# Softplus in one function behind attention, and a conversion of weights whose clamp and add may run on GpSimd or VectorE

## The chip, the core and the metric

The kernel runs on one core of a Trainium2 chip. The core has TensorE (PE: matrix products, with weight loads shown apart as PEld), VectorE (DVE), ScalarE (ACT), GpSimd (POOL) and SyncE (SP), each with its own in-order queue; they wait for each other through semaphores. SP issues most DMAs, POOL a few. [...] The metric is the device time of one execution in microseconds, as the median of the runs.

## The reference

Three layers follow one another. Attention has 4 batches, 8 heads, 576 positions, head size 64, and a mask by blocks of 64. The first experts map 2304 rows of 512 to 2048 features and back, with a softplus between. The second experts normalize by the root mean square, make a gate and a value of 1536 features each, and map silu(gate) x value back to 512.

```python
scores = scale * np.matmul(q, k.transpose(0, 1, 3, 2))      # scale = 1/8
scores = np.where(mask, scores, -1000000000.0)
scores = scores - np.max(scores, axis=-1, keepdims=True)
attn = np.exp(scores)
attn = attn / (np.sum(attn, axis=-1, keepdims=True) + 1e-09)
x = attn @ v
...
h = x @ w_in
g = np.maximum(h, 0.0) + np.log1p(np.exp(-np.abs(h)))
y = g @ w_out
...
rms = np.sqrt(np.mean(y * y, axis=-1, keepdims=True) + 1e-06)
xn = y / rms * rms_g
g = xn @ w_gate
silu = g * (1.0 / (1.0 + np.exp(-g)))
out = (silu * (xn @ w_val)) @ w_out
```

## The kernel before, in words

**Stages.** The rows are cut into 6 blocks of 384, the 2048 features into 16 pieces of 128 (f), of which 9 (NA) belong to stage A and 7 to stage B, since the converted weights of 16 pieces don't fit beside attention's buffers. Stage A runs f = 0 to 8 for all blocks and is mixed with attention, block by block. Stage B, behind it, runs f = 9 to 15 for all blocks, 42 steps, adds what stage A left, takes the mean square and the reciprocal root of each row (`evac_b`), and stores the block. Then come the second experts: `load_xn` loads and normalizes a block, `g34` makes the products and the gate, `g5` the map back.

**Precision.** Products of the first experts and most of attention take a high and a low part of each operand, three products for one. Attention's first 12 of 48 units (`whole(u)`) take full fp32 operands instead: there k is used as loaded (`k0`), the score's maximum is scaled by 1/8 by an operation of its own (L769), and Exp scales by 1/8 (`s_exp`, L791).

**Conversion of weights.** They arrive as 64-bit words. `to_fp32` turns 128x512 of them into fp32 bits in six instructions: Abs of the high word (ACT, L470), conversion of the low word to an integer (ACT, L471), a clamp from below (DVE, L472), shift and mask (DVE, L464), the sign (DVE, L468), and the integer add of the low part (POOL, L475). It is done 68 times: 32 for the first experts' pieces (`w_unit`), 24 for gate and value (`gv_unit`), 12 for the last map (`o_pair`).

**Softplus.** `g1` makes h in a PSUM bank; then Abs (ACT, L963, from PSUM), Exp (L964), Ln of 1 + e (L965), and max(h, 0) + e on DVE (L966, from the same bank). The high part is copied by ACT (L331), the low part is a difference on DVE (L341); `g2` multiplies them three steps later (LAG). `evac_b` takes the root with Ln and Exp (L1030, L1031).

**What sets the order.** Nothing runs in the order of the code. `Plan` collects the operations with an engine, a cost, a key and their reads and writes; `schedule` walks through them, each engine taking the ready operation of the lowest key, and `emit` writes them in the order of their planned start. Where an operation lists several engines (`op2`, `aop2`, `small`), the planner takes the one that ends first by its costs. So a new cost or a new choice moves instructions on all engines. `after=` names operations that must have started before. ACT's functions lie in tables: a function outside the loaded one brings an ACT_TABLE_LOAD in front of it. Before, one table serves Abs, Copy, Square, Exp and Ln up to the first Silu.

## Time and profile before

| | us |
|---|---|
| median of 3 runs (lowest, highest) | 1015.72 (1014.25, 1019.61) |
| the profiled execution, its span | 1021.46, 1019.7 |
| PE busy in the span | 966.8 (95%) |
| DVE, ACT, POOL busy | 799.8 (78%), 658.2 (65%), 277.3 (27%) |
| weight loads busy | 841.0 (82%) |
| mean granted TensorE clock | 0.983 of full speed |

A busy share is a mean over stages with different limits. Attention and stage A reach to about 440 us, stage B to about 590, where the last of its steps overlap the first of the second experts; behind 640 us only these run. Idle time of an engine costs something only where the others wait for it; PE has the least.

### The profile page before, as it was taken

How to read it: one execution, taken by the hardware profiler on the slowest of the kernel's cores; microseconds unless marked ns; L12 is line 12 of the kernel's file. 1: busy time of each engine (PE TensorE's matmuls, PEld its weight loads, DVE VectorE, ACT ScalarE, POOL GpSimd, SP SyncE). 2: the span in 40 equal slices, each digit the busy share in tenths (PEclk: the TensorE clock that was granted, in tenths of full speed). 3: DMA queues.
4: the chain of work that ended last, by engine and by line, in shares of the span. 5: the costliest groups of instructions: out<-in, count | busy, mean ns of one | idle time of the engine just before them, and what ended most of it. 6: DMA issues, size and time to landing. Idle time of an engine off the chain costs nothing.

```text
span 1019.7 us, 20047 instructions
## 1 busy us (share of the span) xinstructions
PE 966.8 (95%) x7438; PEld 841.0 (82%) x7438; DVE 799.8 (78%) x1819; ACT 658.2 (65%) x1491; POOL 277.3 (27%) x353
## 2 busy tenths in 40 slices
PE   6888998899999999999999966999999999999998
PEld 4576887789899999999999966678778788788785
DVE  6889987788989858788687999899888754545545
ACT  7898776587878858787677776465565544333332
POOL 3544432222233303342322536232222110000000
PEclk9999999999999999999999989899999999999999
DMA  7354699999875442555664436052511200035422
GB/s 275 128 177 149 176 263 225 225 271 234 250 174 151 101 102 101 186 192 205 235 245 176 139 115 234 22 197 86 179 56 71 73 1 32 11 105 190 162 72 84
DMA packets 123315, 154.80 MB, mean 152 GB/s; under 512 B 85840, under 2 KB 93776, under 8 KB 121168
## 3 DMA queue, kind: packets, MB, share of 16 engines
q1 hardware_dynamic: 122640, 147.22, 47.9%
q0 software_dynamic: 576, 6.29, 1.7%
q8 instruction: 58, 0.95, 0.4%
q14 instruction: 41, 0.34, 0.1%
HBM read 101.19 MB, written 31.85 MB: 130 GB/s over the span
## 4 chain that ended last, share of the span: by engine, by line
PE 73%; DVE 10%; DMA 8%; ACT 6%; issue 2%; SPq 0%; POOL 0%; ACTq 0%; DVEq 0%
PE b L438 73%; DMA wraw<-in_w2gv_dram 3%; DMA wraw<-in_w_dram 2%; DMA raw<-in_vP_dram 1%; DMA raw<-in_kT_dram 1%; DVE pst L816 1%; DVE nm L757 1%; ACT P L791 1%; DVE g L341 1%; DVE w L551 1%; ACT P L835 1%; DVE t L966 1%; DMA pt<-pst 1%; DVE wa L468 1%; DVE tops L510 1%
## 5 line engine op out<-in xcount | busy, mean ns | idle before, releaser
L438 PE MATMUL b<-x,w 128*128 128x192 f16 (+1 forms) x4176 | 491.9, 273 | 14.2 <-ACT m L1106 6.1
L438 PEld LDWEIGHTS <-w 128*128 128x128 f16 x3024 | 252.7, 98 | 22.8 <-issue 14.1
L438 PE MATMUL b<-g,w 128*128 128x384 f32 x1152 | 234.3, 346 | 7.3 <-DVE g L341 3.6
L438 PEld LDWEIGHTS b<-g,w 128*128 128x128 f32 x1152 | 204.5, 192 | 13.0 <-DVE g L341 5.6
L438 PEld LDWEIGHTS b<-x,w 128*128 128x128 f32 x1152 | 199.6, 188 | 7.5 <-DVE nm L799 1.2
L438 PE MATMUL b<-w,g 128*128 128x512 f16 x648 | 147.6, 383 | 0.0
L438 PEld LDWEIGHTS <-g 128*128 128x128 f16 x648 | 63.4, 99 | 69.7 <-issue 2.4
L1106 ACT COPY m<-b 128x384 f32<-128x384 f32 x108 | 51.2, 477 | 81.9 <-PE b L438 81.7
L791 ACT ACTIVATE P<-b,nm 128x288 f32<-128x288 f32 (+8 forms) x160 | 79.7, 500 | 27.8 <-DVE nm L757 7.3
L1095 DVE TENSOR_TENSOR m<-m 128x384 f32<-128x384 f32 x64 | 37.9, 592 | 68.9 <-ACT m L1106 68.2
L475 POOL TENSOR_TENSOR wa<-wa,wraw 128x512 int32<-128x512 int32 x44 | 63.8, 1450 | 88.9 <-DVE wa L468 51.7
L757 DVE TENSOR_REDUCE nm<-b 128x1 f32<-128x288 f32 (+8 forms) x160 | 70.6, 449 | 16.1 <-PE b L438 14.2
L438 PE MATMUL b<-khl,qbd 128*128 128x448 f32 (+7 forms) x360 | 69.5, 314 | 4.4 <-ACT P L791 3.7
L341 DVE TENSOR_TENSOR g<-t,g 128x384 fp32r<-128x384 f32 x96 | 65.5, 684 | 8.5 <-ACT g L331 8.2
L816 DVE SCALAR_TENSOR_TENSOR pst<-P,nm,pst 128x128 f16<-128x128 f32 (+4 forms) x108 | 66.3, 626 | 3.3 <-ACT pst L813 2.5
L966 DVE SCALAR_TENSOR_TENSOR t<-b,t 128x384 f32<-128x384 f32 x96 | 52.7, 551 | 18.0 <-ACT t L965 17.6
L963 ACT ACTIVATE t<-b 128x384 f32<-128x384 f32 x96 | 46.8, 490 | 30.9 <-PE b L438 30.7
L438 PEld LDWEIGHTS b<-khl,qbd 128*128 128x128 f32 x360 | 57.1, 190 | 7.9 <-ACT P L791 5.4
L331 ACT CAST g<-t 128x384 fp32r<-128x384 f32 x96 | 48.9, 513 | 14.5 <-DVE t L966 11.1
L475 POOL TENSOR_TENSOR wg<-wg,wraw 128x512 int32<-128x512 int32 x24 | 34.3, 1431 | 87.3 <-DVE wg L468 67.0
L964 ACT ACTIVATE t<-t 128x384 f32<-128x384 f32 x96 | 50.4, 528 | 1.4
L965 ACT ACTIVATE t<-t 128x384 f32<-128x384 f32 x96 | 50.3, 527 | 1.2
(133 smaller groups left out, 1404.7 us busy)
## 6 DMA issues: line engine op xcount, KB each, us to landing
wraw<-in_w2gv_dram SPq DMA_DIRECT2D x48, 512.0 KB, 4.0
wraw<-in_w_dram SPq DMA_DIRECT2D x32, 512.0 KB, 3.3
wraw<-in_w2o_dram SPq DMA_DIRECT2D x24, 512.0 KB, 3.4
yd<-y SPq DMA_DIRECT2D x12, 768.0 KB, 4.1
y<-yd SPq DMA_DIRECT2D x12, 768.0 KB, 5.0
qf<-in_qP_dram SPq DMA_DIRECT2D x42, 192.0 KB, 3.1
xd<-x SPq DMA_DIRECT2D x4, 1536.0 KB, 7.4
x<-xd POOLq DMA_DIRECT2D x4, 1536.0 KB, 7.7
```

What stands on the lines that cost most here:

```text
L331: "ACT": ("ACT", t_act(n), lambda: nc.scalar.copy(dst(), src())),
L341: "DVE": ("DVE", t_dve(n), lambda: nc.vector.tensor_tensor(dst(), a(), b(), ALU.subtract)),
L438: nc.tensor.matmul(o, lhsT=l, rhs=r, start=start, stop=stop, **kw)
L475: op("POOL", t_pool2(CW), prio, lambda: nc.gpsimd.tensor_tensor(a().bitcast(I32), a().bitcast(I32), lw().bitcast(I32), ALU.add), [cell, (r ...
L757: aop("DVE", t_dve(cn), key, lambda sp=sp, col=col, cn=cn: nc.vector.tensor_reduce(nm()[:, col:col + 1], sp()[:, :cn], axis=AX.X, op=ALU.m ...
L791: aop("ACT", 0.24 + cn * 0.836e-3, key, lambda sp=sp, col=col, c0=c0, cn=cn: nc.scalar.activation(P()[:, c0:c0 + cn], sp()[:, :cn], ACTF.E ...
L816: aop("DVE", t_dve(c, True), key, lambda: nc.vector.scalar_tensor_tensor(lo(), pc(), r(), hi(), ALU.mult, ALU.subtract), [P, (P, "pad"), ( ...
L963: op("ACT", t_act(BLK, False), key - 5, lambda: nc.scalar.activation(e(), h()[:, :BLK], ACTF.Abs), [h], [e])
L964: op("ACT", t_act(BLK), key - 5, lambda: nc.scalar.activation(e(), e(), ACTF.Exp, scale=-1.0), [e], [e])
L965: op("ACT", t_act(BLK), key - 5, lambda: nc.scalar.activation(e(), e(), ACTF.Ln, bias=1.0), [e], [e])
L966: op("DVE", t_dve(BLK), key - 5, lambda: nc.vector.scalar_tensor_tensor(e(), h()[:, :BLK], 0.0, e(), ALU.max, ALU.add), [h, e], [e])
L1106: op("ACT", t_act(BLK, False), key + 1, lambda o=o, s=s: nc.scalar.copy(s(), ps(o)()), [o], [s])
```

## The change

Softplus, one function, stands in stage B in place of Abs, Exp, Ln and L966; stage A keeps them. It lies in another table, without Abs, Exp and Ln; so `evac_b` loads the table of Ln and Exp in front of its root and the next Softplus loads its own again, and a conversion that is planned for stage B takes the absolute value as a bitwise AND on DVE (`plain`). The first Softplus may start only when all Exps have. In `to_fp32` the clamp may go to POOL or DVE, and the add to POOL or DVE. For attention's first units k is scaled by 1/8 when it has come, and the scaling of the maximum and of Exp goes. Two single-column operations (L700, L799) may go to POOL too. In all, the order has 35 clamps on POOL and 33 on DVE, 28 adds on POOL and 40 on DVE, 38 ANDs on DVE and 30 Abs on ACT, 42 Softplus, 58 of 144 norms (L799, now L808) on POOL, and 14 table loads where there were 2.

```diff
@@ -449,6 +449,7 @@
...
     w_units = {}
+    plain = [0]
 
@@ -467,12 +468,21 @@
...
 
-        op("ACT", t_act(CW), prio, lambda: nc.scalar.activation(a(), hw().bitcast(FP32), ACTF.Abs), [raw], [cell])
         op("ACT", t_act(CW), prio, lambda: nc.scalar.activation(lw().bitcast(I32), lw(), ACTF.Copy, scale=2.0**-29), [raw], [(raw, "l")])
-        op("DVE", t_dve2(CW), prio, lambda: nc.vector.tensor_scalar(a(), a(), 2.0**-15, None, ALU.max), [cell], [cell], port=True)
+        if plain[0]:
+            op("DVE", t_dve2(CW), prio, lambda: nc.vector.tensor_scalar(a().bitcast(U32), hw(), 0x7FFFFFFF, None, ALU.bitwise_and), [raw], [cell])
+        else:
+            op("ACT", t_act(CW), prio, lambda: nc.scalar.activation(a(), hw().bitcast(FP32), ACTF.Abs), [raw], [cell])
+        op2([
+            ("POOL", t_pool(CW), lambda: nc.gpsimd.tensor_scalar(a(), a(), 2.0**-15, 2.0**-15, ALU.max, ALU.max)),
+            ("DVE", t_dve2(CW), lambda: nc.vector.tensor_scalar(a(), a(), 2.0**-15, None, ALU.max)),
+        ], prio, [cell], [cell], port=True)
         op("DVE", t_dve2(CW), prio, shift, [cell], [cell], port=True)
         op("DVE", t_dve(CW), prio, sign, [cell, raw], [cell], port=True)
-        op("POOL", t_pool2(CW), prio, lambda: nc.gpsimd.tensor_tensor(a().bitcast(I32), a().bitcast(I32), lw().bitcast(I32), ALU.add), [cell, (raw, "l")], [cell])
+        op2([
+            ("POOL", t_pool2(CW), lambda: nc.gpsimd.tensor_tensor(a().bitcast(I32), a().bitcast(I32), lw().bitcast(I32), ALU.add)),
+            ("DVE", t_dve(CW), lambda: nc.vector.tensor_tensor(a().bitcast(I32), a().bitcast(I32), lw().bitcast(I32), ALU.add)),
+        ], prio, [cell, (raw, "l")], [cell])
 
@@ -636,6 +646,7 @@
...
         att_ops.append(load(key, lambda: k0(p), kT[0, p], writes=[k_cell(p)], nbytes=294912))
+        aop2([("ACT", t_act(S), lambda: nc.scalar.mul(k0(p), k0(p), 0.125)), ("POOL", t_pool(S), lambda: nc.gpsimd.tensor_scalar(k0(p), k0(p), 0.125, 1.0, ALU.mult, ALU.mult))], key, [k_cell(p)], [k_cell(p)])
 
@@ -697,7 +708,7 @@
...
         aop("DVE", 0.07, key, lambda: nc.vector.tensor_scalar(dsc[p], am()[:, 1:2], 2.0**-28, None, ALU.mult), [am], [("dsc", p)])
-        aop("DVE", 0.07, key, lambda: nc.vector.tensor_scalar(am()[:, 2:3], am()[:, 1:2], 2.0**-14, None, ALU.mult), [am], [(am, "r")])
+        small(("POOL", "DVE"), lambda e: e.tensor_scalar(am()[:, 2:3], am()[:, 1:2], 2.0**-14, 1.0, ALU.mult, ALU.mult), key, [am], [(am, "r")])
         aop("DVE", 0.08, key, lambda: nc.vector.reciprocal(am()[:, 2:3], am()[:, 2:3]), [(am, "r")], [(am, "r")])
@@ -765,8 +776,6 @@
...
                 todo, i0, i1 = [done[-1]], ib, ib + 1
-            cells = [(nm, i) for i in range(i0, i1)]
-            small(("DVE", "POOL"), lambda e: e.tensor_scalar(nm()[:, i0:i1], nm()[:, i0:i1], 0.125, 1.0, ALU.mult, ALU.mult), key, cells, cells)
         else:
@@ -783,12 +792,12 @@
...
         P = part[u, ib] = R_P.new()
-        scale = 0.125 if whole(u) else 1.0
         if n % 128:
...
             col = 4 + ib + c
-            aop("ACT", 0.24 + cn * 0.836e-3, key, lambda sp=sp, col=col, c0=c0, cn=cn: nc.scalar.activation(P()[:, c0:c0 + cn], sp()[:, :cn], ACTF.Exp, scale=scale, bias=nm()[:, ib:ib + 1], accum_out=nm()[:, col:col + 1]), [sp, (nm, ib)], [P, (nm, "s", ib)])
+            exp_op.append(len(plan.ops))
+            aop("ACT", 0.24 + cn * 0.836e-3, key, lambda sp=sp, col=col, c0=c0, cn=cn: nc.scalar.activation(P()[:, c0:c0 + cn], sp()[:, :cn], ACTF.Exp, bias=nm()[:, ib:ib + 1], accum_out=nm()[:, col:col + 1]), [sp, (nm, ib)], [P, (nm, "s", ib)])
         if len(chunks) == 2:
@@ -796,7 +805,7 @@
...
         cells = [(nm, "s", i) for i in range(i0, i1)]
-        small(("DVE",), lambda e: e.tensor_scalar(nm()[:, 8 + i0:8 + i1], nm()[:, 4 + i0:4 + i1], 1e-9, 1.0 if whole(u) else 2.0**-14, ALU.add, ALU.mult), key, cells, [(nm, "t", i0)])
+        small(("DVE", "POOL"), lambda e: e.tensor_scalar(nm()[:, 8 + i0:8 + i1], nm()[:, 4 + i0:4 + i1], 1e-9, 1.0 if whole(u) else 2.0**-14, ALU.add, ALU.mult), key, cells, [(nm, "t", i0)])
         aop("DVE", 0.08, key, lambda: nc.vector.reciprocal(nm()[:, 12 + i0:12 + i1], nm()[:, 8 + i0:8 + i1]), [(nm, "t", i0)], [(nm, "r", i) for i in range(i0, i1)])
@@ -945,7 +954,9 @@
...
 
-    def g1(j, f, key):
+    exp_op, sp_op = [], []
+
+    def g1(j, f, key, soft=False):
         w, x, h = w_units["w1", f], x_b[j], R_h.new()
@@ -960,10 +971,15 @@
...
         g_b[j, f] = g
-        op("ACT", t_act(BLK, False), key - 5, lambda: nc.scalar.activation(e(), h()[:, :BLK], ACTF.Abs), [h], [e])
-        op("ACT", t_act(BLK), key - 5, lambda: nc.scalar.activation(e(), e(), ACTF.Exp, scale=-1.0), [e], [e])
-        op("ACT", t_act(BLK), key - 5, lambda: nc.scalar.activation(e(), e(), ACTF.Ln, bias=1.0), [e], [e])
-        op("DVE", t_dve(BLK), key - 5, lambda: nc.vector.scalar_tensor_tensor(e(), h()[:, :BLK], 0.0, e(), ALU.max, ALU.add), [h, e], [e])
+        if soft:
+            op("ACT", t_act(BLK, False) + (1.28 if not sp_op else 0.0), key - 5, lambda: nc.scalar.activation(e(), h()[:, :BLK], ACTF.Softplus), [h], [e], after=sp_op[-1:] or exp_op)
+            sp_op.append(len(plan.ops) - 1)
+        else:
+            op("ACT", t_act(BLK, False), key - 5, lambda: nc.scalar.activation(e(), h()[:, :BLK], ACTF.Abs), [h], [e])
+            op("ACT", t_act(BLK), key - 5, lambda: nc.scalar.activation(e(), e(), ACTF.Exp, scale=-1.0), [e], [e])
+            exp_op.append(len(plan.ops))
+            op("ACT", t_act(BLK), key - 5, lambda: nc.scalar.activation(e(), e(), ACTF.Ln, bias=1.0), [e], [e])
+            op("DVE", t_dve(BLK), key - 5, lambda: nc.vector.scalar_tensor_tensor(e(), h()[:, :BLK], 0.0, e(), ALU.max, ALU.add), [h, e], [e])
         op2(copies(nc, BLK, lambda: g()[:, 0], e, ("ACT",)), key - 2, [e], [(g, 0)])
@@ -1027,8 +1043,13 @@
...
         op("DVE", t_dve(BLK), key, lambda: nc.vector.tensor_scalar(ms(), o()[:, :BLK], 1.0 / DM, 1e-6, ALU.mult, ALU.add), [o], [ms])
-        op("ACT", t_act(BLK), key, lambda: nc.scalar.activation(rs(), ms(), ACTF.Ln), [ms], [rs])
-        rs_op[:] = [op("ACT", t_act(BLK), key, lambda: nc.scalar.activation(rs(), rs(), ACTF.Exp, scale=-0.5), [rs], [rs])]
+
+        def root():
+            nc.scalar.preload_act_table_set("natural_log_exp_and_others")
+            nc.scalar.activation(rs(), ms(), ACTF.Ln)
+            nc.scalar.activation(rs(), rs(), ACTF.Exp, scale=-0.5)
+
+        rs_op[:] = [op("ACT", 2 * t_act(BLK) + 2.56, key, root, [ms], [rs])]
         pair2(key, t, rs, rs, ALU.mult, [rs], [t])
@@ -1112,7 +1133,7 @@
...
         e1 = R_t.new()
-        op("ACT", t_act(BLK, False) + 0.09 + (1.28 if first else 0.0), key + 2, lambda: nc.scalar.activation(e1(), ps(A)(), ACTF.Silu, scale=fac(3)), [A, ("f", 3)], [e1], after=rs_op if first else ())
+        op("ACT", t_act(BLK, False) + 0.09 + (1.28 if first else 0.0), key + 2, lambda: nc.scalar.activation(e1(), ps(A)(), ACTF.Silu, scale=fac(3)), [A, ("f", 3)], [e1], after=rs_op + sp_op[-1:] if first else ())
         val1, gate2 = R_t.new(), s7
@@ -1272,6 +1293,7 @@
...
     t_b = win[NB] + LAG * step
+    plain[0] = 1
     for i, f in enumerate(range(NA, NF1)):
@@ -1307,7 +1329,7 @@
...
                 load_x(order[n + 1], key_b(s))
-            g1(j, f, key_b(s))
+            g1(j, f, key_b(s), True)
         if LAG <= s < n_b + LAG:
@@ -1333,6 +1355,7 @@
...
                 if i0 == 0 and 0 < n < len(late):
+                    plain[0] = 0
                     w2_unit(late[n], R_wB, key)
```

ACT in stage B, two steps of the activation before (t is the step's tile, b its bank; L471 and L331 are parts of the conversion and the high copy).

```order
L963 ACTIVATE t<-b_5998 128x384
L964 ACTIVATE t<-t 128x384
L965 ACTIVATE t<-t 128x384
L470 ACTIVATE wg<-wraw 128x512
L963 ACTIVATE t<-b_6019 128x384
L331 CAST g<-t 128x384
L964 ACTIVATE t<-t 128x384
L471 ACTIVATE wraw<-wraw 128x512
L965 ACTIVATE t<-t 128x384
L331 CAST g<-t 128x384
```

The same engine and place now, with the first table load of Softplus.

```order
L975 ACT_TABLE_LOAD
L975 ACTIVATE t<-b_5741 128x384
L471 ACTIVATE wraw<-wraw 128x512
L331 CAST w<-wa 128x512
L331 CAST g<-t 128x384
L975 ACTIVATE t<-b_5758 128x384
L331 CAST w<-wa 128x512
L331 CAST g<-t 128x384
L975 ACTIVATE t<-b_5780 128x384
L331 CAST g<-t 128x384
```

One instruction per step reads the bank where one of ACT and one of DVE did, and Abs of the conversion (L470) is gone from ACT.

ACT at the last block's root, before the first Silu (L1115, now L1136), before.

```order
L470 ACTIVATE wg<-wraw 128x512
L471 ACTIVATE wraw<-wraw 128x512
L1030 ACTIVATE r<-r 128x384
L1031 ACTIVATE r<-r 128x384
L1115 ACT_TABLE_LOAD
L1115 ACTIVATE t<-b_7698,fac 128x384
```

And now.

```order
L471 ACTIVATE wraw<-wraw 128x512
L560 ACTIVATE w<-wa,fac 128x512
L1048 ACT_TABLE_LOAD
L1049 ACTIVATE r<-r 128x384
L1050 ACTIVATE r<-r 128x384
L1136 ACT_TABLE_LOAD
L1136 ACTIVATE t<-b_7557,fac 128x384
```

A second load stands in front of the root; the one before Silu was there.

DVE behind the normalization of the first block of the second experts (L1052, now L1073, is a low part of it, L551, now L561, a weight's), before.

```order
L1052 TENSOR_TENSOR x<-y,x 128x384 x2
L472 TENSOR_SCALAR wa<-wa 128x512
L1011 TENSOR_TENSOR y<-y 128x2x192
L464 TENSOR_SCALAR wa<-wa 128x512
L551 SCALAR_TENSOR_TENSOR w<-wg,fac,w 128x256
L468 SCALAR_TENSOR_TENSOR wa<-wraw,wa 128x512
L1052 TENSOR_TENSOR x<-y,x 128x384
L472 TENSOR_SCALAR wa<-wa 128x512
L551 SCALAR_TENSOR_TENSOR w<-wg,fac,w 128x512
L464 TENSOR_SCALAR wa<-wa 128x512
```

And now (L473 is the AND, L478 the clamp, L465 the shift, L469 the sign, L484 the add).

```order
L473 TENSOR_SCALAR wa<-wraw 128x512
L1027 TENSOR_TENSOR y<-y 128x2x192
L478 TENSOR_SCALAR wa<-wa 128x512
L1073 TENSOR_TENSOR x<-y,x 128x384 x2
L465 TENSOR_SCALAR wa<-wa 128x512
L1027 TENSOR_TENSOR y<-y 128x2x192
L469 SCALAR_TENSOR_TENSOR wa<-wraw,wa 128x512
L561 SCALAR_TENSOR_TENSOR w<-wa,fac,w 128x512
L1073 TENSOR_TENSOR x<-y,x 128x384
L484 ISA wa<-wraw,wa 128x1024
L473 TENSOR_SCALAR wa<-wraw 128x512
L561 SCALAR_TENSOR_TENSOR w<-wg,fac,w 128x1024
```

The AND and the add have come into DVE's row, with the add written over 128x1024 half words; here the clamps stay on DVE.

## Rows read from the trace of the kernel before

**Rows 1.** Stretches: length, busy PE, PEld, DVE, ACT, POOL, clock, DMA share, GB/s.

```profile
30.00:100.00 70.00, 60.92 (x356) 47.51 (x355) 60.34 (x171) 63.79 (x156) 30.68 (x40) 0.97 0.46 154
100.00:300.00 200.00, 186.72 (x1401) 171.50 (x1400) 172.40 (x524) 147.09 (x393) 61.83 (x114) 0.98 0.91 227
...
440.00:570.00 130.00, 130.00 (x744) 128.93 (x744) 104.86 (x187) 98.06 (x194) 42.09 (x37) 1.00 0.57 203
570.00:602.00 32.00, 26.69 (x137) 24.99 (x136) 30.45 (x46) 24.34 (x48) 17.76 (x15) 0.95 0.47 161
602.00:638.00 36.00, 23.84 (x211) 21.32 (x210) 34.85 (x52) 22.45 (x42) 18.76 (x14) 0.90 0.55 191
638.00:1019.70 381.70, 376.56 (x3480) 298.19 (x3479) 261.20 (x456) 172.60 (x335) 49.42 (x42) 0.99 0.26 89
```

**Rows 2.** Waits of PE, 570 to 645 us: total us, times, longest.

```profile
PE b L438 <- DVE g L341: 2.4, 2, 2.1
PE b L438 <- ACT g L331: 2.4, 1, 2.4
```

**Rows 3.** Groups on ACT: busy us, mean ns | idle before, releaser.

```profile
L965 ACT ACTIVATE t<-t 128x384 f32<-128x384 f32 x96 | 50.3, 527 | 1.2
...
L963 ACT ACTIVATE t<-b 128x384 f32<-128x384 f32 x96 | 46.8, 490 | 30.9 <-PE b L438 30.7
...
L470 ACT ACTIVATE wa<-wraw 128x512 f32<-128x512 f32 x44 | 29.8, 677 | 8.4 <-DMA wraw<-in_w_dram 5.1 <-DMA wraw<-in_w2o_dram 2.7 <-DVE w L551 0.4
...
L677 ACT ACTIVATE khl<-raw 128x576 fp32r<-128x576 f32 x12 | 8.2, 684 | 7.8 <-DMA raw<-in_kT_dram 7.6
```

**Rows 4.** Groups on DVE, same columns.

```profile
L341 DVE TENSOR_TENSOR g<-t,g 128x384 fp32r<-128x384 f32 x96 | 65.5, 684 | 8.5 <-ACT g L331 8.2
...
L966 DVE SCALAR_TENSOR_TENSOR t<-b,t 128x384 f32<-128x384 f32 x96 | 52.7, 551 | 18.0 <-ACT t L965 17.6
...
L551 DVE SCALAR_TENSOR_TENSOR w<-wg,fac,w 128x256 f16<-128x256 f32 (+2 forms) x36 | 34.2, 953 | 4.1 <-ACT w L550 4.1
...
L472 DVE TENSOR_SCALAR wa<-wa 128x512 f32<-128x512 f32 x44 | 23.9, 543 | 6.7 <-ACT wa L470 6.1
...
L468 DVE SCALAR_TENSOR_TENSOR wg<-wraw,wg 128x512 uint32<-128x512 uint32 x24 | 20.0, 834 | 0.1
...
L769 DVE TENSOR_SCALAR nm<-nm 128x1 f32<-128x1 f32 x28 | 3.9, 146 | 0.1
```

**Rows 5.** ACT in time, 631 to 635 us: start, us, operation [idle before].

```profile
631.56 0.52 ACT L1030 ACTIVATE r<-r 128x384 f32<-128x384 f32 x1 [2.34 <-DVE r L1029]
...
632.66 1.28 ACT L1115 ACT_TABLE_LOAD   x1
633.95 0.58 ACT L1115 ACTIVATE t<-b,fac 128x384 f32<-128x384 f32 x1
```

**Rows 6.** Groups with shapes kept apart, DVE and POOL.

```profile
L551 DVE SCALAR_TENSOR_TENSOR w<-wg,fac,w 128x1024 f16<-128x1024 f32 x12 | 15.4, 1280 | 4.1 <-ACT w L550 4.1
...
L811 POOL TENSOR_SCALAR pst<-P,nm 128x512 f16<-128x512 f32 x12 | 9.3, 778 | 23.2 <-DVE nm L800 17.9 <-ACT t L963 3.2 <-ACT g L331 1.8
```

**Rows 7.** Groups on POOL.

```profile
L475 POOL TENSOR_TENSOR wa<-wa,wraw 128x512 int32<-128x512 int32 x44 | 63.8, 1450 | 88.9 <-DVE wa L468 51.7 <-DVE wa L464 6.3 <-ACT m L1106 5.9
...
L769 POOL TENSOR_SCALAR nm<-nm 128x1 f32<-128x1 f32 x8 | 3.0, 380 | 10.1 <-DVE nm L759 3.5 <-DVE nm L800 2.4 <-DVE nm L757 2.0
```

**Rows 8.** DVE in time, 180 to 215 us: start, us.

```profile
194.09 1.68 DVE L709 SCALAR_TENSOR_TENSOR vhl<-raw,am,vhl 128x640 f16<-128x640 f32 x1
...
207.03 0.87 DVE L709 SCALAR_TENSOR_TENSOR vhl<-raw,am,vhl 128x640 f16<-128x640 f32 x1
```

**Rows 9.** POOL in time, same stretch.

```profile
194.09 1.00 POOL L342 TENSOR_TENSOR qbd<-qf,qbd 128x384 fp32r<-128x384 f32 x1 [1.06 <-ACT qbd L331]
```

**Rows 10.** Waits of all engines up to 100 us.

```profile
ACT P L791 <- DVE nm L769: 4.4, 5, 3.4
PE b L438 <- DMA qf<-in_qP_dram: 4.3, 1, 4.3
```

## The prediction

> **What bounds the kernel now.** I read the stretches of the run first, then what TensorE (PE) waits for in the stretches where it idles, then what one instruction of each kind takes. The table of stretches [rows 1] splits the run by stage. From 440 to 570 us (stage B, the second part of the first experts) PE is busy 130.00 of 130.00 us and from 638 us to the end 376.56 of 381.70, so there another engine's time is worth nothing unless it comes to bind. What is open behind the start lies in two places: 9.1 us of PE idle from 30 to 100 us and 13.3 up to 300 us (attention, run beside stage A), and 5.3 + 12.2 = 17.5 us from 570 to 638 us (the change from the first experts to the second, called the transition below). In that last place VectorE (DVE) is busy 30.45 of 32 and 34.85 of 36 us: it is the bound there, with ScalarE (ACT) at 76% and 62%. Among PE's waits there [rows 2], 2.4 + 2.4 us are for the two halves of an activated g, the end of the chain that the change shortens. From 30 to 100 us ACT is the fullest engine, 63.79 of 70 us.
>
> **The change part by part.** The profiled execution took 1021.46 us, 5.74 above the median of the runs, 1015.72. The sum is made on the former and its difference taken off the latter.
>
> *Softplus.* Each of the 42 steps of stage B loses Exp and Ln on ACT (0.527 us for L965, the row of L964 is alike) and the max-and-add L966 on DVE (0.551); Softplus reads the same 128x384 of PSUM as Abs did and is priced as that, 0.490 [rows 3, 4]. That is 42 x 1.054 = 44.3 us of ACT and 42 x 0.551 = 23.1 us of DVE. Nearly all of it lies beside a PE that is 100% busy, so I cost it at 0 there: the cover is PE's own work, and it is gone only from 570 us on, where the last steps' chain is exposed. The first Softplus has to start behind the last Exp of stage A; PE gives ACT the steps in that order anyway: 0.
>
> *Tables.* The order has 14 table loads where 2 were: Softplus, back to Ln and Exp for each block's root, and Softplus again. Each is 1.28 us, and the next function starts at its end (load at 632.66, Silu at 633.95) [rows 5]. 12 x 1.283 = 15.4 us of ACT, so ACT still gains 29 us. Behind a root's load stand two functions and the next Softplus; in stage B the steps behind have a full PE queue ahead of them. At the last block the load stands in front of a wait of 2.34 us for DVE [rows 5], which hides it: 0, or +1.3 if that wait goes.
> [...]
>
> *Conversion of weights.* There are 68. The clamp (0.543 on DVE, L472) goes to GpSimd (POOL) in 35; on POOL the nearest row is another one-input operation over 128x512, 0.778 [rows 6]. The integer add (1.450 on POOL, L475 [rows 7]) goes the other way in 40. On DVE no row shows it. From below: 0.543, a one-input operation of the length; from above: 1.280, an operation over the 128x1024 that the order writes for it [rows 6]. The nearest in kind is L468, two inputs, one of them the same strided raw: 0.834 [rows 4], which I take. Its net price is lower, even below nothing: a two-input operation on POOL holds DVE up. L709 takes 0.87 alone and 1.68 with L342 of 1.00 beside it [rows 8, 9], so an add that leaves POOL gives DVE back up to 0.81; the range of the net is -0.3 to +1.3. In 38 conversions Abs leaves ACT (0.677, L470 [rows 3]) for a bitwise AND on DVE, which I price as the clamp, 0.543 (0.834 if the strided read costs it).
> [...]
>
> *The transition*, from the seventh-last step of stage B to the second block's normalization (L1046), counted in the order. DVE loses 8 L966 (-4.4), 6 clamps (-3.3), 4 differences at L341's 0.684 (-2.7), 3 weight splits at L551's 0.953 (-2.9) that now stand elsewhere, a shift priced as L472 and a sum priced as L966 (-1.1); it gains 11 ANDs (+6.0), 7 adds (+5.8) and two priced as L341 (+1.4): -1.2 [rows 4]. POOL's two-input operations fall from 34 to 23; at 0.6 of stretch each, three quarters of the 0.81 above, DVE gets 6.6 back, and gives 7 x 0.4 = 2.8, half their length, for the clamps there. DVE has 5.0 us less in the stretch that it bounds. ACT loses 8 x 1.05 + 12 x 0.677 and gains 4 loads, -11.4, which also ends the two waits of 2.4 us. I take -5. What is late next is DVE's queue itself: the normalization of the first block of the second experts stands behind the conversions. From below: -12, two thirds of the idle; from above: +7, worked out with the third rival.
>
> *Attention.* Scaling k by 1/8 once per head pair puts four ACT operations of 128x576 (0.684, L677) at the start and takes 36 single-column scales off (28 on DVE at 0.146, 8 on POOL at 0.380) [rows 3, 4, 7]. The first product waits for q until 4.3 us [rows 10]; k lands somewhat before, so of 0.684 and a handoff I take +0.5 (0 to +0.9). In return the step between maximum and Exp is gone, for which ACT waited 4.4 us in five places [rows 10]. Up to 100 us there are 18 conversions: DVE loses 10 clamps and gains 12 adds, loses 28 scales and 13 norms: -5.4 + 10.0 - 4.1 - 1.9 = -1.4; POOL loses 12 adds of 1.45, and with them a stretch of DVE. I take -2 of the 9.1 us (-4 to +3). The sums' norm (priced as L769, 0.146) goes to POOL in 58 places at 0.380. Behind it on POOL stand the split's first half and k's and q's halves, and the reciprocal on DVE waits for it: +0.23 a piece, 13 if all were on the path; but POOL is 31% busy from 100 to 300 us, and DVE loses some 6.6 us. I take -1 (-4 to +4).
>
> **Sum:** +0.5 - 2 - 1 + 0 - 5 = -7.5 us, 1013.96 against 1021.46, or 1008.2 against the median: **1008 us**.
>
> **The rivals.**
> *No difference (1015).* From 570 to 638 us DVE binds, its own work falls by only 1.2 us, and the stretch by POOL may not fall as I take it: one two-input operation of POOL gives way to another. Then the transition gives 0 and attention -1 to 0. For it: DVE's busy share there. Against it: the two waits for g. 32%.
> *Much faster (1000).* DVE gives up 18 us in stage B, where it is 81% busy, so that conversions run ahead and the transition closes by 12 us, the first 100 us by 4, less 0.5 for the start: 15.5 off. Against it: the order has 11 conversions in the transition where 12 stood, so little has run ahead. 12%.
> *Slower (1027).* The add on DVE is as long as its 1024 elements say, 1.28, and the AND pays for its strided read, 0.83. The place is the transition, where DVE has no room: 9.0 + 9.2 for these, 5.4 for POOL's clamps at full stretch and the 1.4, against the 14.4 taken off and half of the stretch given back, 3.3: about +7. In the first 100 us 12 x 1.28 - 11.4 = +4, of which 3 counts, and the start +0.7: +11 in all. It decides over the gain from about 1.0 us for the add. For it: the row of 128x1024. Against it: the add has 512 words to give, as L468. 18%.
>
> **How the numbers follow.** Forecast 38%, with its own range of 1003 to 1011; no difference 32%; much faster 12%; slower 18%. About 0.5%, 5 us, is what a measurement of this kernel can tell from no change: under 1010.6 is faster, over 1020.8 slower. The forecast and the large gain give 0.50 for faster, less 0.01 for the forecast's upper edge; no difference and that edge 0.33; slower 0.18. The range goes from 1000, the large gain, to 1021, and leaves out half of that gain's cases and most of the slower ones.
>
> **What would show it.** Right: Softplus rows of 0.49 us x42 with 14 table loads of 1.28; PE still 100% busy in stage B; the waits of PE for g in the transition gone, and PE idle there 12 us rather than 17.5; the add on DVE at 0.8 us; fewer long rows among DVE's two-input operations. Wrong: the add over 1.0 us, DVE full and PE's idle after 570 us the same or more; PE idle between 100 and 440 us above 13.5 us, which would make the new order of attention, and not the named edits, decide.

## The result, and the profile after

The changed kernel takes 1020.74 us (median of 9 executions, 1016.66 to 1025.91) against 1014.25 (9, 1012.51 to 1019.61): ratio 1.0057, 95% interval [1.0037, 1.0078]. It is slower, by 0.6%; 1008 and "faster" were forecast. The time lies in the range, 0.3 us under an upper end that stood for other reasons, which is luck; the direction is wrong. The executions scatter by some 4 us either way: the profiled one after, 1016.66, is the fastest of its nine, and the one before, 1021.46, lies above all nine of its kernel. So the spans of these two (1014.9 and 1019.7) say nothing on the change; what is read here is durations and waits, and the time lost is placed by kernels that share one order. One execution below, at 1038.02, is over 1.5% above the fastest of its kernel (experiment 2) and is left out of that kernel's median, which is 1028.7 with it.

Groups on all engines after: busy us, mean ns | idle before, releaser. They answer to [rows 3, 4, 6, 7].

```profile
L477 POOL TENSOR_SCALAR wa<-wa 128x512 f32<-128x512 f32 x22 | 45.6, 2075 | 48.3 <-DVE wa L473 24.3 <-ACT wa L475 17.9 <-DVE m L1116 6.2
...
L477 POOL TENSOR_SCALAR wg<-wg 128x512 f32<-128x512 f32 x13 | 27.9, 2145 | 52.7 <-DVE wg L473 36.2 <-ACT wg L475 16.4
...
L483 POOL TENSOR_TENSOR wa<-wa,wraw 128x512 int32<-128x512 int32 x16 | 23.4, 1459 | 24.4 <-DVE wa L469 6.3 <-issue 5.4 <-ACT g L1151 4.6
...
L465 DVE TENSOR_SCALAR wa<-wa 128x512 uint32<-128x512 uint32 x44 | 21.2, 482 | 16.2 <-POOL wa L477 16.0
...
L975 ACT ACTIVATE t<-b 128x384 f32<-128x384 f32 x42 | 20.4, 486 | 22.4 <-PE b L438 21.4 <-POOL r L1027 0.9
...
L808 POOL TENSOR_SCALAR nm<-nm 128x1 f32<-128x1 f32 x58 | 17.7, 306 | 53.1 <-ACT P L800 46.0 <-PE b L438 3.5 <-DVE nm L802 1.2
...
L473 DVE TENSOR_SCALAR wa<-wraw 128x512 uint32<-128x512 uint32 x22 | 13.7, 622 | 1.3 <-DMA wraw<-in_w_dram 0.9
...
L478 DVE TENSOR_SCALAR wa<-wa 128x512 f32<-128x512 f32 x22 | 9.4, 429 | 2.5 <-ACT wa L475 2.3
...
L975 ACT ACT_TABLE_LOAD x6 | 7.7, 1283 | 0.1
L1048 ACT ACT_TABLE_LOAD x6 | 7.7, 1283 | 0.1
```

Softplus (0.486), the loads (1.283), the add on DVE (L484, 0.829, 23.2 us in 28 for the tiles wa) and the AND (0.622 here, 0.439 in the 16 others) cost what was forecast. One does not: the clamp on POOL, L477, takes 2.08 and 2.15 us where 0.778 was priced. Behind it DVE's shift (L465) waited 16.0 us in 17 places, and 6.6 more for the second kind of tile; before, the shift on these tiles (L464) stood behind 0.3 us of idle.

Stretches after, columns as in [rows 1]; the last row is the transition whole.

```profile
30.00:100.00 70.00, 62.51 (x378) 48.42 (x376) 59.36 (x161) 64.30 (x162) 34.94 (x45) 1.00 0.45 151
100.00:440.00 340.00, 330.25 (x2435) 309.77 (x2435) 292.72 (x798) 245.57 (x628) 135.42 (x235) 0.99 0.73 194
440.00:560.00 120.00, 117.86 (x669) 116.01 (x668) 88.76 (x161) 66.46 (x115) 36.69 (x32) 1.00 0.58 207
560.00:640.00 80.00, 62.32 (x421) 57.27 (x420) 73.48 (x120) 48.31 (x86) 42.16 (x30) 0.89 0.45 156
```

The same two stretches before, cut alike:

```profile
100.00:440.00 340.00, 326.51 (x2405) 305.51 (x2404) 286.25 (x825) 254.17 (x653) 105.30 (x175) 0.99 0.73 188
...
560.00:640.00 80.00, 61.67 (x411) 57.37 (x410) 76.82 (x117) 56.66 (x107) 43.33 (x32) 0.92 0.47 162
```

In the transition PE idles 17.7 us where it idled 18.3: the 5 us forecast there did not come. Its waits after, 560 to 640 us (total, times, longest):

```profile
PE b L438 <- ACT m L1127: 9.9, 2, 9.2
PE b L438 <- ACT x L1072: 4.6, 1, 4.6
PE b L438 <- DVE m L1114: 2.7, 1, 2.7
```

The two waits for g [rows 2] are gone, as forecast. A wait for ACT's eviction `m`, 5.1 us at its longest before, is 9.2 us in their place. The line of before, same stretch (L1106 is now L1127):

```profile
PE b L438 <- ACT m L1106: 6.1, 3, 5.1
```

### The profile page after: what moved, and what is told of

Same layout as the page of the kernel before. It is cut to its first block, busy times and chain, and to the rows that moved or that the text cites. A ratio compares the mean times of both kernels' runs of the same rounds, so it can differ in the third digit from the quotient of the medians.

```text
span 1014.9 us, 19866 instructions
## 1 busy us (share of the span) xinstructions
PE 961.8 (95%) x7438; PEld 838.9 (83%) x7438; DVE 783.6 (77%) x1735; ACT 611.8 (60%) x1370; POOL 320.5 (32%) x412
## 5 line engine op out<-in xcount | busy, mean ns | idle before, releaser
L438 PE MATMUL b<-g,w 128*128 128x384 f32 x1152 | 230.6, 341 | 0.5 <-DVE g L341 0.3
L438 PEld LDWEIGHTS b<-g,w 128*128 128x128 f32 x1152 | 200.7, 189 | 4.8 <-DVE g L341 1.7
L1127 ACT COPY m<-b 128x384 f32<-128x384 f32 x108 | 51.0, 477 | 71.4 <-PE b L438 71.2
L341 DVE TENSOR_TENSOR g<-t,g 128x384 fp32r<-128x384 f32 x96 | 61.0, 638 | 11.5 <-ACT g L331 11.0
L331 ACT CAST g<-t 128x384 fp32r<-128x384 f32 x96 | 49.1, 512 | 26.1 <-PE b L438 20.2
L477 POOL TENSOR_SCALAR wa<-wa 128x512 f32<-128x512 f32 x22 | 45.6, 2075 | 48.3 <-DVE wa L473 24.3
L471 ACT ACTIVATE wraw<-wraw 128x512 int32<-128x512 uint32 x68 | 46.1, 682 | 15.0 <-DMA wraw<-in_w2gv_dram 8.2
L477 POOL TENSOR_SCALAR wg<-wg 128x512 f32<-128x512 f32 x13 | 27.9, 2145 | 52.7 <-DVE wg L473 36.2
L822 ACT ACTIVATE pst<-P,nm 128x384 f16<-128x384 f32 (+4 forms) x60 | 35.9, 604 | 13.0 <-DVE nm L809 6.8
L342 POOL TENSOR_TENSOR wg<-wg 128x256 f32<-128x256 f32 x30 | 27.4, 913 | 50.3 <-DVE w L561 45.0
L1114 DVE TENSOR_TENSOR m<-b,m 128x384 f32<-128x384 f32 x72 | 39.6, 549 | 3.8 <-PE b L438 3.8
```

The costliest lines, as they stand in the source:

```text
L331: "ACT": ("ACT", t_act(n), lambda: nc.scalar.copy(dst(), src())),
L341: "DVE": ("DVE", t_dve(n), lambda: nc.vector.tensor_tensor(dst(), a(), b(), ALU.subtract)),
L438: nc.tensor.matmul(o, lhsT=l, rhs=r, start=start, stop=stop, **kw)
L471: op("ACT", t_act(CW), prio, lambda: nc.scalar.activation(lw().bitcast(I32), lw(), ACTF.Copy, scale=2.0**-29), [raw], [(raw, "l")])
L477: ("POOL", t_pool(CW), lambda: nc.gpsimd.tensor_scalar(a(), a(), 2.0**-15, 2.0**-15, ALU.max, ALU.max)),
L822: "ACT": ("ACT", t_act(c) + 0.09, lambda: nc.scalar.activation(hi(), pc(), ACTF.Copy, scale=r())),
```

## The experiments

Each time is the median of 5 to 12 executions; ratios are to the kernel before on the same chip, whose medians lay between 1014.7 and 1015.3 us (1014.25 for the first row).

| run | order | clamp on POOL, us | time, us | ratio [95%] |
|---|---|---|---|---|
| changed kernel | C | 2.08, 2.15 | 1020.7 | 1.0057 [1.0037, 1.0078] |
| 6 max, times 1.0 | C | 2.11, 2.11 | 1020.1 | 1.0051 [1.0030, 1.0072] |
| 5 one max | C | 1.66, 1.69 | 1010.3 | 0.9953 [0.9937, 0.9970] |
| 1 product | C | 0.75, 0.83 | 1005.6 | 0.9910 [0.9891, 0.9928] |
| 3 no Softplus | N | 2.11, 2.08 | 1021.1 | 1.0060 [1.0038, 1.0082] |
| 8 same, one max | N | 1.68, 1.64 | 1013.6 | 0.9972 [0.9955, 0.9988] |
| 7 same, product | N | 0.77, 0.77 | 1006.8 | 0.9919 [0.9894, 0.9945] |
| 10 clamp alone, one max | P | 1.66, 1.67 | 1026.3 | 1.0116 [1.0080, 1.0152] |
| 15 same, product | P | 0.81, 0.73 | 1021.7 | 1.0066 [1.0045, 1.0087] |
| 2 clamp on DVE only | own | none | 1027.8 | 1.0116 [1.0085, 1.0146] |
| 9 order alone | own | none | 1013.5 | 0.9984 [0.9962, 1.0005] |
| 4 Softplus alone | own | none | 1021.2 | 1.0047 [1.0029, 1.0065] |
| 13 AND alone | own | none | 1021.1 | 1.0066 [1.0032, 1.0100] |
| 11 add alone | own | none | 1006.7 | 0.9913 [0.9896, 0.9930] |
| 12 add, Softplus | own | none | 1007.7 | 0.9925 [0.9901, 0.9948] |
| 16 add, norms | own | none | 1009.8 | 0.9955 [0.9932, 0.9978] |
| 14 add, scaling, norms | own | none | 1025.0 | 1.0096 [1.0061, 1.0132] |
| 17 as 5, no scaling of k | own | 1.65, 1.62 | 1021.4 | 1.0072 [1.0047, 1.0097] |

Rows with the same letter have one and the same order on every engine (C is the changed kernel's); only POOL's clamp differs. The others were planned anew. A product in the clamp's place (1, 7, 15) leaves the clamp out of those conversions: these three kernels price its length and do not replace it.

**The clamp's length, order held.** My theory after the result: the clamp is the loss. Experiment 1, in L477, with 5 and 6 beside it:

```diff
-nc.gpsimd.tensor_scalar(a(), a(), 2.0**-15, 2.0**-15, ALU.max, ALU.max)
+nc.gpsimd.tensor_scalar(a(), a(), 1.0, 1.0, ALU.mult, ALU.mult)       # 1
+nc.gpsimd.tensor_scalar(a(), a(), 2.0**-15, None, ALU.max)            # 5
+nc.gpsimd.tensor_scalar(a(), a(), 2.0**-15, 1.0, ALU.max, ALU.mult)   # 6
```

Expected of 1:

> The changed kernel in exactly its order on every engine; only the instruction that the 35 clamps on GpSimd issue is another: times 1.0 times 1.0 in place of the larger of two constants (these 35 conversions go without their clamp). First theory (the clamp on GpSimd takes 2.1 us where 0.78 was priced, VectorE's shift waits for it and conversions end late): the rows of L477 fall to 0.66 to 0.78 us, the 22.6 us of waits of VectorE behind it to under 8, and the time to 1008 to 1014. Rival (the new order, with its scaling of k and its reloaded tables, costs the time whatever the clamp takes): the rows fall likewise, the time stays at 1017 to 1022.

Expected of 5:

> The changed kernel in exactly its order; the clamp on GpSimd is one function (the larger of the value and the constant, nothing behind it) where it was two; the result is the same. If each maximum costs GpSimd a pass of its own: rows of L477 about 1.3 to 1.5 us, time 1009 to 1015. If a maximum is slow on GpSimd however many there are: rows 1.9 to 2.2, time 1017 to 1023. If only the pair is slow: rows 0.66 to 0.78, time 1004 to 1009.

Expected of 6:

> The changed kernel in exactly its order; the clamp on GpSimd is the larger of value and constant, then times 1.0; the result is the same. If one maximum costs a slow pass and a product a fast one: rows of L477 between those of a single maximum and 1.7 us, time 1010 to 1016. If the pair of function kinds decides and any maximum makes it slow: 1.9 to 2.2 us, time 1017 to 1023. If a product behind it is what makes it fast: 0.66 to 0.78 us, 1004 to 1009.

Groups of experiment 1, then of 5, then of 6:

```profile
L465 DVE TENSOR_SCALAR wa<-wa 128x512 uint32<-128x512 uint32 x44 | 20.0, 455 | 1.6 <-POOL wa L477 1.3
...
L477 POOL TENSOR_SCALAR wa<-wa 128x512 f32<-128x512 f32 x22 | 16.6, 754 | 50.6 <-ACT wa L475 26.2 <-DVE wa L473 24.4
...
L477 POOL TENSOR_SCALAR wg<-wg 128x512 f32<-128x512 f32 x13 | 10.8, 830 | 51.4 <-DVE wg L473 34.6 <-ACT wg L475 16.8
```

```profile
L477 POOL TENSOR_SCALAR wa<-wa 128x512 f32<-128x512 f32 x22 | 36.6, 1663 | 49.3 <-ACT wa L475 24.9 <-DVE wa L473 20.8 <-ACT g L331 3.5
...
L477 POOL TENSOR_SCALAR wg<-wg 128x512 f32<-128x512 f32 x13 | 22.0, 1691 | 49.3 <-DVE wg L473 32.9 <-ACT wg L475 16.3
```

```profile
L477 POOL TENSOR_SCALAR wa<-wa 128x512 f32<-128x512 f32 x22 | 46.4, 2109 | 48.5 <-DVE wa L473 24.4 <-ACT wa L475 24.2
```

With a product in its place, L477 takes 0.75 to 0.83 us, the price I had forecast, and the kernel takes 1005.6: 15.1 us less by that one instruction, and 9.7 under the kernel before. That is under the 1008 to 1014 that I expected of 1. One maximum takes 1.66; a second function behind it, a maximum or times 1.0, adds 0.4. So of my readings of 5 the first holds roughly (a slow pass), of 6 the second: the maximum is what is slow, and a product behind it doesn't help. The time follows: the first 0.9 us of clamp cost 4.7, the next 0.43 cost 10.

How it reaches PE, in the trace of the changed kernel from 83 us on (start, us, engine, operation [idle before]):

```profile
83.50 2.12 POOL L477 TENSOR_SCALAR wa<-wa 128x512 f32<-128x512 f32 x1 [0.87 <-ACT wa L475]
...
85.66 0.43 DVE L465 TENSOR_SCALAR wa<-wa 128x512 uint32<-128x512 uint32 x1 [1.48 <-POOL wa L477]
...
86.00 1.04 DVE L341 TENSOR_TENSOR w<-wa,w 128x512 fp32r<-128x512 f32 x1
...
86.97 0.68 DVE L469 SCALAR_TENSOR_TENSOR wa<-wraw,wa 128x512 uint32<-128x512 uint32 x1
...
87.57 0.54 DVE L982 SCALAR_TENSOR_TENSOR t<-b,t 128x384 f32<-128x384 f32 x1
...
88.17 1.55 PE L438 MATMUL b<-raw,pst 128*128 128x288 f32 x4 [0.95 <-DVE t L982]
```

and the same sixth clamp in experiment 1:

```profile
78.16 0.62 POOL L477 TENSOR_SCALAR wa<-wa 128x512 f32<-128x512 f32 x1 [0.45 <-ACT wa L475]
...
78.81 0.43 DVE L465 TENSOR_SCALAR wa<-wa 128x512 uint32<-128x512 uint32 x1 [0.22 <-POOL wa L477]
...
80.12 0.68 DVE L469 SCALAR_TENSOR_TENSOR wa<-wraw,wa 128x512 uint32<-128x512 uint32 x1
...
81.29 0.56 DVE L982 SCALAR_TENSOR_TENSOR t<-b,t 128x384 f32<-128x384 f32 x1 [0.49 <-ACT t L981]
...
81.90 1.55 PE L438 MATMUL b<-raw,pst 128*128 128x288 f32 x4
```

DVE's operations start in the order of its queue (85.66 to 87.57 us). The shift stands at its head and waits 1.48 us for POOL; behind it stands L982, which frees a PSUM bank, and PE waits 0.95 us for that. With the short clamp the shift waits 0.22 and PE not at all. At this clamp experiment 1 is already 5.3 us ahead (78.16 against 83.50), after five earlier ones.

PE runs the same 7438 instructions in both traces, so their starts can be laid side by side. The changed kernel is 2.8 us behind at 33 us and 7.5 at 139 us; this falls to 5.1 by 300 us, within the stretch (106 to 381 us) in which POOL has no clamp, and ends at 9.9. That is less than the 15.1 us between the medians: the trace after is the fastest of its nine executions. In the sums over the two traces (the changed kernel's, then experiment 1's; length, then busy time of each engine) PE's idle falls from 53.1 us to 45.3:

```profile
sum 1014.89, PE 961.79 PEld 838.91 DVE 783.55 ACT 611.83 POOL 320.52; mean PE 160.30 PEld 139.82 DVE 130.59 ACT 101.97 POOL 53.42
```

```profile
sum 1004.94, PE 959.62 PEld 839.63 DVE 780.31 ACT 612.49 POOL 277.36; mean PE 159.94 PEld 139.94 DVE 130.05 ACT 102.08 POOL 46.23
```

**The same in two other orders.** Experiments 3, 7 and 8 put the three functions of stage B back and leave out the root's table; 10 and 15 are the kernel of 9 with only the choice of POOL for the clamp.

Expected of 3:

> The changed kernel with Abs, Exp, Ln and the sum back in stage B, no bitwise AND, and the root without a table of its own; clamp, add, scaling of k and norms as changed. First theory (the clamp on GpSimd is the cost, Softplus a gain of some us): 1020 to 1026, no faster than the changed kernel. Rival (Softplus and its 12 added table loads are the cost): 1008 to 1015.

Expected of 7:

> The kernel of the third experiment (changed kernel without Softplus) in exactly that order, with GpSimd's clamp replaced by times 1.0 (those conversions go without their clamp). First theory (the clamp's length is the loss in either, Softplus a gain of 2 to 8 us once conversions are in time): rows of L477 at 0.66 to 0.78 us, time 1008 to 1014, over the 1005.6 of the first experiment. Rival (Softplus is worth nothing): 1004 to 1007. Rival (it is the order without Softplus that is late for other reasons): 1017 to 1022.

Expected of 8:

> The kernel of the third experiment (changed kernel without Softplus), in that order, GpSimd's clamp as one maximum (1.66 us in the fifth experiment); the result is the same. The third and the seventh (2.1 us: 1021.1, 0.75 us: 1006.8) leave 10.6 us per 1.35 us of clamp, if the time is even in it: 1006.8 + 0.9 x 10.6 / 1.35 x ... = 1013 to 1015. If only what exceeds some cover costs (first the short, then the long waits): 1009 to 1013, as with Softplus (1010.3). If Softplus is worth something with a clamp of this length: at least 3 us above 1010.3.

Expected of 10:

> The kernel of the experiment 'order alone' plus the choice of GpSimd for the clamp, as one maximum of 1.66 us, nothing else of the change. Theory (VectorE is short between 30 and 640 us, so a clamp off it is a gain as long as its length is hidden): 1008 to 1013. Rival (the gain of the short clamp came from the add's or the scaling's freedom, not from the clamp's): equal to 'order alone' within 3 us.

Expected of 15:

> The kernel of 'clamp alone' (1026.3) in exactly its order, GpSimd's 32 clamps as times 1.0 (these conversions go without their clamp; 0.7 to 0.85 us in place of 1.66). If the length is the loss: 32 x 0.85 = 27 us less on GpSimd, and by the 5 us per 0.9 us of the first and fifth experiments 1019 to 1023; if all the loss against 'order alone' is length: 1010 to 1015. If the order is the loss: 1024 to 1028.

The length is worth 14.3 us in order N (2.1 us to the product) and 4.6 in P (1.66 to the product). Softplus is worth little at any of three lengths: 1020.7 with it against 1021.1, 1010.3 against 1013.6, 1005.6 against 1006.8, each pair in two orders. The middle pair just meets the 3 us that I had set for a worth of Softplus, but its ratios, 0.9953 and 0.9972, have intervals that overlap. In my expectation of 8 a sum is wrong: 1021.1 less 1006.8 is 14.3, not 10.6, and a time even in the length would then give 1016. At 1013.6 the time is not even in it, as in order C. That its tables are the cost (the rival of experiment 3) falls. Experiment 10 went against my expectation by 13 us, and 15 shows that most of it is not the length: 1021.7 is still 8 over "order alone".

**The parts, planned anew.**

```diff
-            ("POOL", t_pool(CW), lambda: nc.gpsimd.tensor_scalar(a(), a(), 2.0**-15, 2.0**-15, ALU.max, ALU.max)),
...
-            ("DVE", t_dve(CW), lambda: nc.vector.tensor_tensor(a().bitcast(I32), a().bitcast(I32), lw().bitcast(I32), ALU.add)),
...
-        aop2([("ACT", t_act(S), lambda: nc.scalar.mul(k0(p), k0(p), 0.125)),
...
-            g1(j, f, key_b(s), True)
+            g1(j, f, key_b(s))
```

The first line goes in 2, 4, 9, 11 to 14 and 16 (clamp on DVE); the second in 4, 9, 10, 13 and 15 (add on POOL); the scaling in 4, 9 to 13 and 15 to 17, where the scale of the maximum and of Exp comes back; Softplus in 3, 7 to 11 and 13 to 16. The norms are back on DVE in 4, 9 to 13 and 15. In 13, `plain` stays 1 without Softplus.

Expected of 2:

> The changed kernel with the choice of GpSimd for the clamp taken away, and the order planned anew: 68 clamps on VectorE at 0.43 to 0.54 us. First theory (GpSimd's clamp is the cost): 1007 to 1013, below the kernel before. Rival (Softplus with its table loads, or the scaling of k, is the cost): 1016 to 1022. A second rival (VectorE is full, so 35 clamps more of 0.43 us there cost as much as they did on GpSimd): 1015 to 1021 with more waits of PE on VectorE between 300 and 640 us.

Expected of 4:

> The kernel before with the Softplus part alone: Softplus in stage B, the root with its own table, the bitwise AND in place of Abs for the conversions of stage B; clamp on VectorE, add on GpSimd, no scaling of k, norms on VectorE. First theory (Softplus is a gain, the clamp on GpSimd the loss): 1007 to 1013. Rival (Softplus and its table loads are the loss): 1017 to 1023. No effect of Softplus: 1013 to 1016.

Expected of 9:

> None of the change's operations: clamp on VectorE, add on GpSimd, no Softplus, no scaling of k, norms on VectorE. What is left is that in a conversion the copy of the low word stands ahead of Abs and the root is planned as one step; the planner makes another order from it. If the order in itself moves the time by no more than a measurement can tell: 1012 to 1018. If a new order alone is worth as much as the 5 to 6 us by which the second to fourth kernels differ from the one before: 1019 to 1023, and then the fourth experiment's loss is not Softplus's.

Expected of 11:

> The kernel of the experiment 'order alone' plus the choice between GpSimd and VectorE for the add, nothing else of the change. Theory (VectorE is short; with the clamp on it too, adds of 0.83 us cost there): 1018 to 1028, above 'order alone' by 3 us or more. Rival (the add's freedom is a gain of its own, 1.45 us on GpSimd against 0.83): 1008 to 1013.

Expected of 12:

> The kernel of 'add alone' (1006.7) plus the Softplus part (Softplus in stage B, root with its own table, 38 bitwise ANDs on VectorE in place of Abs on ScalarE); clamp on VectorE, no scaling of k, norms on VectorE. If Softplus with its AND is what loses where the clamp stays on VectorE (order alone 1013.5, Softplus alone 1021.2): 1012 to 1018, or up to the second experiment's 1028.7. If scaling and norms lose there: 1003 to 1008.

Expected of 13:

> The kernel of 'order alone' (1013.5) with one edit: the conversions planned for stage B take the absolute value as a bitwise AND on VectorE, as they must beside Softplus, but Softplus isn't there and no table changes. If the AND on VectorE is what makes 'Softplus alone' slower (1021.2): 1017 to 1023. If Softplus's table loads and its place in the order do it: 1011 to 1016.

Expected of 14:

> The kernel of 'add alone' (1006.7) plus the scaling of k and the norms that may go to GpSimd; no Softplus, clamp on VectorE. If scaling and norms are worth what was forecast (0.5 us lost at the start, some 3 us gained in attention): 1003 to 1007. If they take the add's gain away: 1012 to 1022.

Expected of 16:

> The kernel of 'add alone' (1006.7) plus the norms that may go to GpSimd, without the scaling of k. If the scaling of k (first scores 4 us later, attention planned another way from there) takes the gain away: 1004 to 1010. If the norms on GpSimd do (in its queue behind adds of 1.45 us, so that maps of attention wait): 1018 to 1027.

Expected of 17:

> The changed kernel with the clamp on GpSimd as one maximum (fifth experiment, 1010.3) and without the scaling of k, the order planned anew; the result is the same. If the scaling is what loses in attention: 1000 to 1007. If it is neutral and orders differ by chance: 1006 to 1016. If it is a gain: over 1016.

Here my first theory failed: taking the clamp off POOL altogether (2) gives 1027.8, with 10 and 14 the slowest kernels, above all that I had expected of it; 4 lies over my theory for it too, and 14 over both its readings. And the parts do not add up. The add alone gives 1006.7, where I expected a loss, and even the rival no less than 1008; the AND alone costs 7.6 over "order alone" (1021.1, which is also what Softplus alone takes), yet add with Softplus, AND included, costs 1.0 over the add. The scaling of k costs 15 beside add and norms (14 against 16), yet taking it out of experiment 5 costs 11 (17). An edit that is planned anew moved the time by -7 to +15 us here without a sign of its own, and I can't name what in an order decides. What stays open is therefore the worth of each part apart from its order. Every order with a clamp on POOL was also planned with its wrong price: `t_pool(512)` is 0.67 us. An order that knows 2.1 was not run.

The traces show where the time of two orders lies, though. 14 takes 21.7 us more than 11 (spans 1027.7 and 1006.0), and only 4.7 of them are idle of PE (53.0 against 48.3); for the same number of instructions PE is busy 974.7 us against 957.7. The granted clock of PE was 0.50 of full speed in nine stretches of 14 and in five of 11. One stretch of 14 and the sum of the nine, then the sum of the five of 11:

```profile
563.62:573.86 10.24, 8.91 (x24) 6.79 (x23) 9.09 (x14) 9.43 (x20) 4.58 (x3) 0.50 0.66 226
...
sum 58.04, PE 53.22 PEld 43.42 DVE 50.04 ACT 42.96 POOL 20.66; mean PE 5.91 PEld 4.82 DVE 5.56 ACT 4.77 POOL 2.30
```

```profile
sum 23.89, PE 18.18 PEld 15.96 DVE 21.65 ACT 15.14 POOL 6.34; mean PE 3.64 PEld 3.19 DVE 4.33 ACT 3.03 POOL 1.27
```

PE is busy at that clock for 35.0 us more in 14 (53.2 against 18.2). In the changed kernel's trace 22 products of 128x192 take 3.30 us from 600.60 us on, at a mean granted clock of 0.52, and 24 take 2.00 us from 608 us on, at 1.00: 150 against 83 ns, 1.8 times. If half the clock makes PE's work twice as long, an estimate, half of the 35.0, 17.5, is lost by it, about the 17.0 by which PE is busy longer. So two orders can differ by more than their waits.

Five kernels that keep the clamp beat the one before and the changed one: 11 (the add may go to DVE, nothing else; 1006.7), 12 (1007.7), 16 (1009.8), 5 (1010.3) and 8 (1013.6).

## Why the prediction was wrong, by its steps

**The clamp's price is the step that failed**: "on POOL the nearest row is another one-input operation over 128x512, 0.778 [rows 6]". That row is a product. Engine, tile and count of inputs were alike and the function was not, and the function makes 0.75 or 2.1 us. I gave this cost no bounds from both sides, as I did the add, and its one price stands in the rival "slower" as well. In the changed kernel's own order this difference is 15.1 us; with the product's length the kernel takes 1005.6 where I had said 1008. That it comes so near is luck in part, as the next steps show: the transition gave 0.7 us of its 5, and attention and the start 6.5 for 2.5.

One-input operations on POOL are not alike: the product takes 0.75 us (experiment 1), the maximum 1.66 (experiment 5), against 0.43 on DVE (L478). With 46 us more of clamps on POOL (73.5 against 27.4) DVE is busy only 3.3 us longer (783.6 against 780.3), of the 10 by which these two traces differ. So a stretch of DVE's own operations by the clamps can't be most of the cost. The 0.4 us a clamp that the transition's sum gives for it, and the 5.4 in the rival "slower", were my estimates from the clamp's priced length, and no run shows them: these 3.3 us are 0.07 us for each us of longer clamp, where the sum has half. The clamps cost by being waited for: 22.6 us in DVE's queue, 1.8 with the product. They also hold up what stands behind them in POOL's own queue: waits of other engines for POOL's other operations come to 36 us in the changed kernel's trace and 22 in experiment 1's. How the 15.1 us divide between these two ways no run tells.

**The transition, -5: wrong too.** PE's idle from 560 to 640 us went from 18.3 to 17.7, and with the short clamp it is 17.6, so the clamp is not why. I had the load of the last root hidden by a wait of 2.34 us for DVE [rows 5]. ACT in the changed kernel:

```profile
619.82 0.48 ACT L1127 COPY m<-b 128x384 f32<-128x384 f32 x1 [1.25 <-PE b L438]
...
622.31 0.71 ACT L560 ACTIVATE w<-wa,fac 128x512 f16<-128x512 f32 x1
623.03 1.28 ACT L1048 ACT_TABLE_LOAD   x1
624.33 0.52 ACT L1049 ACTIVATE r<-r 128x384 f32<-128x384 f32 x1
624.88 0.52 ACT L1050 ACTIVATE r<-r 128x384 f32<-128x384 f32 x1
625.43 1.28 ACT L1136 ACT_TABLE_LOAD   x1
626.72 0.58 ACT L1136 ACTIVATE t<-b,fac 128x384 f32<-128x384 f32 x1
...
633.14 0.85 ACT L1127 COPY m<-b 128x384 f32<-128x384 f32 x2
```

The wait that was to hide it is gone: the load follows ACT's split at 623.03, and the root and the next eviction stand behind its 1.28. No gap around the two loads is over 0.03 us, so each costs its 1.28 and no more. Between two evictions `m` ACT runs two loads, the root's two operations, and twelve more: 12.8 us, in which PE waits 9.2. The waits for g that Softplus ended were followed by this one.

Above all, the step "DVE has 5.0 us less in the stretch that it bounds" failed. DVE was busy 76.8 us of these 80 before, 73.5 after and 70.3 with the short clamp, and PE's idle stayed at 18.3, 17.7 and 17.6: DVE's busy time is not what set PE's idle here. The two largest sums of waits after, 9.9 and 4.6 us, are for ACT. That the transition can be shorter is shown by experiment 11, without Softplus and in another order; there PE idles 11.4 us in it:

```profile
560.00:640.00 80.00, 68.64 (x502) 62.80 (x501) 75.00 (x128) 58.22 (x112) 31.27 (x24) 0.91 0.47 161
```

**Attention and start, -2.5 together: right in sign, too small.** PE's idle up to 440 us (30, 70 and 340 us of stretches) was 30.3 before; it is 28.0 after and 23.8 with the short clamp. From 100 to 440 us it fell from 13.5 to 9.8, so the sign of being wrong that I had named there did not come. Of the 7.6 us of idle that experiment 1's trace has less than before's (45.3 against 52.9), 6.5 lie here; of the 7.8 that the long clamp adds again, 4.2 lie here, 2.1 in stage B and 1.4 behind 640 us. These are single traces of kernels that scatter by some 4 us.

```profile
30.00:100.00 70.00, 63.76 (x386) 50.48 (x383) 62.62 (x171) 66.81 (x169) 30.68 (x48) 0.96 0.49 162
100.00:440.00 340.00, 331.21 (x2446) 312.58 (x2443) 290.60 (x793) 245.06 (x621) 120.86 (x228) 0.99 0.75 196
440.00:560.00 120.00, 120.00 (x687) 118.94 (x686) 91.43 (x162) 67.34 (x117) 33.29 (x36) 1.00 0.58 204
560.00:640.00 80.00, 62.44 (x450) 54.95 (x449) 70.32 (x119) 46.78 (x84) 33.93 (x29) 0.89 0.41 141
```

These rows are experiment 1's; its first 30 us hold 21.20 us of PE (22.24 before, 19.24 after). **Stage B, 0**: right with the short clamp, 120.00 of 120; with the long one PE idles 2.1 there.

**The rivals.** "Slower" rested on the add at 1.28 and the AND at 0.83: neither is so, the sign came by another way. "No difference" was right on the transition's number, but not for its reason, that DVE binds there.

## What to carry to other kernels

A row prices an operation only if the function is the same too; where only engine and shape agree, as here 0.778 us stood for 2.08, bound the price from both sides. In a kernel whose order a planner makes, judge a piece with the order held and only its length changed; here edits that were planned anew moved the time by up to 15 us, as much as the piece was worth. An operation that is moved to an idle engine inside a chain can cost through the in-order queue that waits for it, however idle its new engine is: POOL was busy 32% of the span here, and DVE's queue waited 22.6 us for its clamps.

## What the runs showed of the hardware

On POOL one input of 128x512 fp32 takes 0.75 to 0.83 us for product and product (experiment 1), 1.66 for one maximum (5), 2.1 for a maximum with a second function, a maximum or times 1.0, behind it (the changed kernel, 6); DVE takes 0.43 for the maximum (L478). The integer add, written on DVE over 1024 half words, takes 0.83 (0.76 in the tiles wg), near L468's 0.834 over 512 words [rows 4], and not the 1.28 of 1024 elements. In 2 and 12 Abs of a conversion stands behind the last Softplus and before the root, and a fifteenth table load stands in front of it (at 612 us in both): the table of Softplus lacks Abs. That it lacks Exp and Ln too no run shows, since every root beside Softplus loads its table by an instruction of its own (L1048, 1.28 us).
